# q in 112-row blocks, the last queries' scores on opposite array quarters, and three raw buffers for q, k and v

## The chip, the cores and the metric

The kernel runs on one core of a Trainium2 chip. The metric is the device time of one execution in microseconds; the median of three runs stands for the kernel. A core has five engines that each work through a list of their own: TensorE (PE, with its weight loads as PEld), VectorE (DVE), ScalarE (ACT), GpSimd (POOL) and SyncE (SP), which here issues every transfer between device memory and on-chip memory. They wait for one another by semaphores. Matmul results land in PSUM, which is divided into banks.

## The reference

Causal attention over 4 batches x 12 heads, 448 queries each, head width 64, followed by a two-layer block with a rational activation ("MoE" in the names), all float32 in the reference; the weights come in as float64.

```python
scores = scale * np.matmul(q, k.transpose(0, 1, 3, 2))      # (4, 12, 448, 448)
scores = np.where(mask, -1000000000.0, scores)
scores = scores - np.max(scores, axis=-1, keepdims=True)
attn = np.exp(scores)
attn = attn / (np.sum(attn, axis=-1, keepdims=True) + 1e-09)
x = (attn @ v).transpose(0, 2, 1, 3).reshape(1792, 768)
h = x @ w_in                                                 # d_ff = 2048
g = (a0 + a1*h + a2*h**2 + a3*h**3) / (1 + |b0|*|h| + |b1|*h**2 + 1e-6)
out = g @ w_out
```

## The kernel before

The kernel has two stages. In the first, attention, the 48 heads are taken in 24 pairs p; both heads of a pair go through together, 64 columns each. In the second the MoE block works through 64 units of tokens x hidden columns. The float64 weights are turned into float32 blocks (items m) already during attention, in small steps between the attention work.

The order of the work is written by hand. The string ORDER lists the tasks of one iteration; a name with `@2` is done for the pair two before the iteration's own, one with `@-1` for the pair one ahead. Each engine gets its instructions in that order, so a task that has to wait holds up what comes behind it on its engine. The tasks that matter here:

- `ld` (`stage_load`, L206 on) loads q and k of a pair, `@-3`: three pairs ahead. k goes in two loads (one a head) of 4 blocks of 112 rows into a tile with two buffers. q goes in four: for each head three blocks of 128 rows (L213), and the last 64 rows (L214) into the half of the partitions that belongs to the head. Its tiles R are two, used in turn, and their other half is cleared once at the start, so that the last 128 rows hold a block-diagonal q.
- `lv` (`stage_load_v`) loads v in three loads (L223 twice, L226) into one of two tiles V, `@1`: for the pair one before the iteration's own. `d` (`stage_d`, L358), which uses it, is `@2`.
- `qk` (`qk_pe`) transposes q and k on TensorE into two PSUM tiles, `@-1`; `qx`, `qy` and `kx`, `ky` copy them out on ScalarE (L253, L262).
- `s.3` (`stage_b_pe` with i = 3, L280) makes the scores of the last 64 queries of both heads in one product over all 128 rows; `s.2`, `s.1` and `s.0` make those of the others, one product for each head over 64 rows, into two banks. `m` subtracts masks and takes the maximum on VectorE (L292), `e` is the exponential on ScalarE (L299), `r` the reciprocal of the sums on VectorE (L310), `n` the normalising on GpSimd (L314).
- `c` transposes the weights of attention (L334), `a` and `v` copy them out (L342 on ScalarE, L344 on VectorE), `dh` and `dl` split the result into two parts (L368, L371).
- `cv` does the weight steps: on GpSimd (L130, L134) for the pair after, on VectorE (L138, L143), and `cv.3` on SP: it stores a finished float32 block (L149) and loads the float64 block after next (L116, L121) into the tile `raw`, which has two buffers. Pairs 1 to 4 do two of VectorE's steps, the later ones one, so that a store and a load come in every iteration at first and in every second one later.

SP's list in an iteration is thus: store and weight load (if any), v, q, k. The program gives each transfer one of eight lanes (`DMAHW0` to `DMAHW7`) in turn, and a transfer waits for the one before it on its lane.

Of the kernel before, what the change touches and what calls it, by code (L numbers as in the profile page):

```python
# [15 lines left out]


ORDER = """
c.1@2 e.3@1 cv.3 qk@-1 lv@1 e.0@1 v.1@2 dh@3 ld@-3 s.3 r@1 a.1@2 dl@3 n.5@1 qy@-1 c.0@2 m.6 kx@-1 n.4@1 ky@-1 s.2
qx@-1 v.0@2 n.0@1 a.0@2 s.1 n.2@1 e.6 m.5 n.1@1 s.0 m.4 d@2 n.3@1 e.5 m.0 n.6@1 m.2 e.4 m.3 cv.0@-1 e.2 m.1 cv.1  # L20
cv.2 e.1
"""
# [5 lines left out]
"""  # L28

TAIL = """  # L30
e.3@1 c.1@2 e.0@1 v.1@2 dh@3 lv@1 r@1 dl@3 a.1@2 n.5@1 n.4@1 c.0@2 xr n.2@1 n.3@1 v.0@2 a.0@2 n.6@1 wh.1.0 p1.0
n.0@1 n.1@1 wl.1.0 d@2 aa.0 da.0 wh.2.0 dz.0 ab.0 wl.2.0 c.1@1 v.1@1 a.1@1 dh@2 dl@2 c.0@1 a.0@1 v.0@1 p1.1 db.0 dy.0
lw.4.0 gh.0 gl.0 wh.0.1 wl.0.1 aa.1 da.1 d@1 p1.2 xl dh@1 dl@1 dz.1 ab.1 wh.1.1 wl.1.1 wh.3.0 lw.2.1 x.13.0 p2.0
lw.3.1 aa.2 lw.5.0 db.1 wl.3.0 dy.1 wh.4.0 wl.4.0
# [3 lines left out]
def kernel(  # L38
# [23 lines left out]
    SCALE = 1.0 / float(D) ** 0.5  # L62
# [141 lines left out]
    raw, K, AT, pv, SUM, REC, psa, pss, psc, nmx = {}, {}, {}, {}, {}, {}, {}, {}, {}, {}  # L204

    def stage_load(p):  # L206
        if p in raw:
            return
        b, hp = divmod(p, HP)
        t = R[p % 2]  # L210
        for j in range(2):
            src = q[b, 2 * hp + j]
            nc.sync.dma_start(out=t[:, :3, j], in_=src[:3 * P].rearrange("(c p) d -> p c d", p=P))  # L213
            nc.sync.dma_start(out=t[half(j), 3, j], in_=src[3 * P:])  # L214
        t = raw[p] = ld.tile([CP, NB, 2, D], F32, tag="k", name="kraw")
        for j in range(2):
            nc.sync.dma_start(out=t[:, :, j], in_=k[b, 2 * hp + j].rearrange("(c p) d -> p c d", p=CP))

    def stage_load_v(p):
        b, hp = divmod(p, HP)  # L220
        t = V[p % 2]
        for j in range(2):
            nc.sync.dma_start(  # L223
                out=t[:, j, :3], in_=v[b, 2 * hp + j, :3 * P].rearrange("(c p) d -> p c d", p=P)
            )
        nc.sync.dma_start(  # L226
            out=t[QB:, :, 3], in_=v[b, 2 * hp:2 * hp + 2, 3 * P:].rearrange("j p d -> p j d")
        )


    def half(j):
        return slice(j * D, (j + 1) * D)

    def ring(x, name):
        return ps_t.tile([P, 512], F32, tag=f"t{x}", bufs=3, name=name)

    def qk_pe(p):
        ps = psa[p] = [ring(x, "psA") for x in range(2)]
        for c in range(4):
            for x in range(2):  # L240
                r = slice(x * QB, (x + 1) * QB)
                nc.tensor.transpose(
                    ps[x][:, c * QB:(c + 1) * QB], R[p % 2][r, c].rearrange("p j d -> p (j d)"), ident[r, r]
                )
        for c in range(NB):
            for x, w in enumerate((QB, CP - QB)):
                r, lo = slice(x * QB, x * QB + w), 4 * QB + c * w
                nc.tensor.transpose(
                    ps[x][:, lo:lo + w], raw[p][r, c].rearrange("p j d -> p (j d)"), ident[r, r]
                )  # L250

    def q_ev(p, x):
        nc.scalar.activation(  # L253
            out=Q[p % 2].rearrange("p (c x r) -> p c x r", c=4, x=2)[:, :, x],
            in_=psa[p][x][:, :4 * QB].rearrange("p (c r) -> p c r", c=4), func=AF.Copy, scale=SCALE,
        )

    def k_ev(p, x):
        if p not in K:
            K[p] = qk.tile([P, S], F32, tag="k", name="kt")  # L260
        lo, hi = x * QB, (QB, CP)[x]
        nc.scalar.copy(  # L262
            out=K[p].rearrange("p (c r) -> p c r", c=NB)[:, :, lo:hi],
            in_=psa[p][x][:, 4 * QB:4 * QB + NB * (hi - lo)].rearrange("p (c r) -> p c r", c=NB),
        )

    b_w = (P, P, 2 * P, 2 * P, 3 * P, 3 * P, S)

    def stage_b_pe(p, i):
        w = b_w[2 * i]  # L270
        if i == 0:
            ps, lo = [pss[p, 2 + j][0] for j in range(2)], 2 * P
        else:
            ps = [ring(x, "psS") for x in range(2)] if i < 3 else [ps_s.tile([P, 512], F32, tag="s3", name="psS")]
            lo = 0
        for j in range(len(ps)):
            o = ps[j][:, lo:lo + w]
            pss[p, 2 * i + j] = (ps[j], o)
            d = half(j) if i < 3 else slice(None)
            nc.tensor.matmul(  # L280
                o, Q[p % 2][d, i * P:(i + 1) * P], K[p][d, :w], start=True, stop=True, skip_group_check=True
            )

    def stage_b_max(p, i):
# [68 lines left out]
    def stage_d(p):  # L353
        ps = pv[p] = ring(0, "psD") if p >= NP - 2 else ps_s.tile([P, 512], F32, tag="d", name="psD")
        a = [AT[p, h].rearrange("p n x q -> p (n x q)") for h in range(2)]
        v = V[p % 2]
        for j, c, h, slot, lo, hi in d_jobs:
            nc.tensor.matmul(  # L358
                ps[half(j), lo * QB:hi * QB], v[:, j, c], a[h][:, slot * QB:(slot + hi - lo) * QB],
                start=(c == 0 and lo == 0), stop=(c == 3), skip_group_check=True,  # L360
            )
# [205 lines left out]
    with tc.manual_schedule():  # L567
# [8 lines left out]
            out=mask[:, 2 * P:3 * P], in_=mask[:, 2 * P:3 * P], compare_op=ALU.is_ge, fill=-1e9, base=0,  # L576
            pattern=[[-1, P]], channel_multiplier=1,
        )
        for j in range(2):
            m = mask[half(j), 3 * P + S - QB:]  # L580
            nc.gpsimd.affine_select(
                out=m, in_=m, compare_op=ALU.is_ge, fill=-1e9, base=0, pattern=[[-1, QB]], channel_multiplier=1,
# [6 lines left out]
        lv = es_l.enter_context(pool(name="lv", bufs=2))  # L589
        ps_t = es_l.enter_context(pool(name="ps_t", bufs=1, space=PSUM))  # L590
        ld = es_r.enter_context(pool(name="ld", bufs=2, side="right"))
        qk = es_r.enter_context(pool(name="qk", bufs=2, side="right"))
        ps_s = es_r.enter_context(pool(name="ps_s", bufs=1, space=PSUM, side="right"))
        for x in ("s3", "d"):
            ps_s.tile([P, 512], F32, tag=x, name="psS")

        Q = [qk.tile([P, 512], F32, tag=f"q{x}", bufs=1, name=f"qt{x}") for x in range(2)]
        R = [ld.tile([P, 4, 2, D], F32, tag=f"q{x}", bufs=1, name=f"qraw{x}") for x in range(2)]
        V = [lv.tile([P, 2, 4, D], F32, tag=f"v{x}", bufs=1, name=f"vraw{x}") for x in range(2)]
        E = [  # L600
            [ep.tile([P, w], F32, tag=f"e{x}{i}", name=f"e{x}{i}") for i, w in enumerate(b_w)]
            for x in range(2)
        ]
# [110 lines left out]
```

## Time and profile before

| | |
|---|---|
| runs | 675.38, 676.63, 669.61 us; median 675.38 |
| the profiled execution | 678.74 us, its span 676.9 us |
| TensorE busy / weight loads | 633.1 us (94%) / 527.5 us (78%) |
| VectorE busy | 536.7 us (79%) |
| ScalarE busy | 427.0 us (63%) |
| GpSimd busy | 207.4 us (31%) |
| moved | 154.98 MB, 229 GB/s over the span |
| loads of q | 48 of 96 KB, 48 of 16 KB |
| loads of k | 48 of 112 KB |
| loads of v | 48 of 96 KB, 24 of 32 KB |
| loads of float64 weights | 32 of 768 KB |

The busy shares are averages over the two stages, which have different limits; what the change touches lies in attention, about the first 194 us. A row of the timeline or of the chain begins with its start and its length in us; a bracket at its end says how long the engine stood before it and for whom. "SPq" rows are the issuing of transfers: their length is that of the issue, not of the transfer.

### The profile page before, as it was taken

The page shows a single profiled execution, that of the slowest core. Times are in us where ns is not written, and L with a number is a line of the kernel's source. Part 1 is how long each engine was busy: PE and PEld are TensorE (multiplying, and loading weights), DVE is VectorE, ACT ScalarE, POOL GpSimd, SP SyncE. Part 2 cuts the span into 40 slices and gives each one's busy share as a digit, 9 for nine tenths or more (in the row PEclk, how much of TensorE's full clock was granted, in tenths as well). Part 3 has the DMA queues.
Part 4 walks back from the last instruction along what each step waited for, and adds up shares of the span by engine and source line. Part 5 has one row for each costly group of instructions (what it writes and reads, how often), then busy time and mean ns, then how long its engine had stood idle before and what let it go on. Part 6 is the DMA issues. An engine that isn't in the chain of part 4 may idle for free.

```text
span 676.9 us, 12813 instructions
## 1 busy us (share of the span) xinstructions
PE 633.1 (94%) x4560; PEld 527.5 (78%) x4560; DVE 536.7 (79%) x1036; ACT 427.0 (63%) x968; POOL 207.4 (31%) x269
## 2 busy tenths in 40 slices
PE   4888988787899998999999999999999999999997
PEld 2555755555577887788887888889999999999996
DVE  1897987887768999999999996866886557786654
ACT  3876987887775665655566656655564555764543
POOL 2667655665565555234355320000000000000000
PEclk9998998999999999999999999999999999999999
DMA  7687767667744898887788698864657785657763
GB/s 181 164 212 176 182 176 190 158 163 207 187 141 170 289 307 312 299 283 280 276 281 319 246 335 310 286 219 171 234 178 262 240 276 193 234 185 251 243 225 116
DMA packets 111679, 154.98 MB, mean 229 GB/s; under 512 B 71936, under 2 KB 84224, under 8 KB 111616
## 3 DMA queue, kind: packets, MB, share of 16 engines
q1 hardware_dynamic: 111616, 154.17, 70.1%
q8 instruction: 36, 0.59, 0.4%
q14 instruction: 27, 0.22, 0.1%
HBM read 117.18 MB, written 36.96 MB: 228 GB/s over the span
## 4 chain that ended last, share of the span: by engine, by line
PE 50%; DVE 27%; DMA 8%; issue 7%; POOL 3%; ACT 2%; SPq 1%; DVEq 0%; POOLq 0%; ACTq 0%
PE psH L196 21%; PE psO L508 16%; PE psM L509 8%; DMA vraw<-in_v_dram 3%; DVE u L138 3%; DVE psS L292 3%; DVE p L468 3%; DMA kraw<-in_k_dram 3%; DVE p L462 3%; DVE w L437 3%; POOL e L314 3%; DVE whl L179 2%; PE psD L358 2%; DVE w L459 2%; PE psS L280 2%
## 5 line engine op out<-in xcount | busy, mean ns | idle before, releaser
L196 PE MATMUL psH<-xh,whl 128*128 128x512 f32 (+1 forms) x768 | 175.9, 364 | 0.5 <-DVE p L445 0.5
L508 PE MATMUL psO<-whl,gh 128*128 128x512 f32 x448 | 160.9, 395 | 3.7 <-ACT gh L474 3.6
L196 PEld LDWEIGHTS psH<-xh,whl 128*128 128x128 f32 x768 | 136.0, 188 | 16.1 <-DVE p L445 0.9
L509 PE MATMUL psM<-whl,gh 128*128 128x256 f32 x448 | 126.2, 282 | 0.0
L508 PEld LDWEIGHTS psO<-whl,gh 128*128 128x128 f32 x448 | 84.0, 188 | 25.9 <-ACT gh L474 8.7
L452 ACT ACTIVATE u<-w,lnb 128x512 f32<-128x512 f32 (+1 forms) x64 | 43.0, 671 | 93.0 <-DVE w L437 93.0
L314 POOL TENSOR_SCALAR e<-e,r 128x384 f32<-128x384 f32 (+3 forms) x168 | 83.0, 516 | 55.4 <-DVE r L310 39.9
L299 ACT ACTIVATE e<-psS,nm 128x256 f32<-128x256 f32 (+3 forms) x168 | 82.6, 505 | 13.6 <-DVE nm L292 11.3
L292 DVE CUSTOM_DVE_ANT_0 psS<-psS,mask 128x128 f32<-128x128 f32 (+3 forms) x168 | 73.6, 473 | 18.7 <-PE psS L280 16.5
L196 PE MATMUL psH<-xl,whl 128*128 128x512 f32 (+1 forms) x384 | 87.4, 362 | 0.0
L509 PEld LDWEIGHTS psM<-whl,gh 128*128 128x128 f32 x448 | 84.5, 189 | 0.9
L508 PE MATMUL psO<-whl,gl 128*128 128x512 f32 x224 | 81.1, 391 | 0.0
L196 PEld LDWEIGHTS psH<-xl,whl 128*128 128x128 f32 x384 | 70.1, 188 | 7.5
L474 ACT CAST gh<-p 128x512 fp32r<-128x512 f32 (+1 forms) x64 | 36.8, 575 | 51.9 <-DVE p L468 51.9
L358 PE MATMUL psD<-at,vraw 128*64 128x64 f32 (+5 forms) x576 | 53.6, 325 | 16.2 <-DMA vraw<-in_v_dram 9.3
L280 PE MATMUL psS<-kt,qt 64*128 64x256 f32 (+3 forms) x336 | 67.3, 438 | 0.7 <-DVE at L344 0.2
L481 DVE TENSOR_TENSOR gl<-p,gh 128x384 fp32r<-128x384 f32 (+1 forms) x62 | 38.2, 616 | 35.1 <-ACT gh L474 35.1
L358 PEld LDWEIGHTS psD<-at,vraw 128*64 128x64 f32 x576 | 38.2, 142 | 32.4 <-ACT e L299 12.7
L509 PE MATMUL psM<-whl,gl 128*128 128x256 f32 x224 | 63.2, 282 | 0.0
L179 DVE TENSOR_TENSOR whl<-w,whl 128x768 fp32r<-128x768 f32 x45 | 45.6, 1014 | 21.4 <-ACT whl L171 20.9
L130 POOL TENSOR_SCALAR raw<-raw 128x768 f32<-128x768 f32 x32 | 38.0, 1186 | 80.2 <-DMA raw<-in_moe_w_in_dram 51.4
L430 ACT ACTIVATE u<-psH 128x512 f32<-128x512 f32 (+1 forms) x64 | 34.3, 535 | 44.0 <-PE psH L196 43.9
(56 smaller groups left out, 1049.2 us busy)
## 6 DMA issues: line engine op xcount, KB each, us to landing
whl<-whl SPq DMA_DIRECT2D x88, 768.0 KB, 4.2
w<-w SPq DMA_DIRECT2D x64, 384.0 KB, 5.1
raw<-in_moe_w_in_dram SPq DMA_DIRECT2D x16, 768.0 KB, 7.1
w<-u SPq DMA_DIRECT2D x32, 384.0 KB, 3.2
raw<-in_moe_w_out_dram SPq DMA_DIRECT2D x16, 768.0 KB, 6.0
kraw<-in_k_dram SPq DMA_DIRECT2D x48, 112.0 KB, 2.6
out_dram<-osb SPq DMA_DIRECT2D x14, 384.0 KB, 2.9
qraw<-in_q_dram SPq DMA_DIRECT2D x48, 96.0 KB, 4.1
```

The costliest lines, as they stand in the source:

```text
L130: nc.gpsimd.tensor_scalar(out=y, in0=y, scalar1=2.0 ** -112, scalar2=1.0, op0=ALU.mult, op1=ALU.mult)
L179: eng.tensor_tensor(out=w[:, 1], in0=src, in1=w[:, 0].bitcast(F32), op=ALU.subtract)
L196: nc.tensor.matmul(ps, w[:, c * P:(c + 1) * P], x[c][:, lo:lo + n_tok], start=(c == 0 and n == 0), stop=(c == KD - 1 and n == 2),)
L280: nc.tensor.matmul(o, Q[p % 2][d, i * P:(i + 1) * P], K[p][d, :w], start=True, stop=True, skip_group_check=True)
L292: nc.vector.tensor_tensor_reduce(out=s, in0=s, in1=m, scale=-1.0, scalar=3e38, op0=ALU.add, op1=ALU.min, accum_out=nmx[p][:, i:i + 1],)
L299: nc.scalar.activation(out=E[p % 2][i][:, :w], in_=pss[p, i][1], func=AF.Exp, bias=nmx[p][:, i:i + 1], scale=-1.0, accum_out=SUM[p][:, i:i ...
L314: nc.gpsimd.tensor_scalar(out=e, in0=e, scalar1=REC[p][:, i:i + 1], scalar2=0.0, op0=ALU.mult, op1=ALU.add)
L358: nc.tensor.matmul(ps[half(j), lo * QB:hi * QB], v[:, j, c], a[h][:, slot * QB:(slot + hi - lo) * QB], start=(c == 0 and lo == 0), stop=(c ...
L452: nc.scalar.activation(out=r, in_=w, func=AF.Ln, scale=2.0 ** -LSH, bias=lnb[:, 0:1])
L481: eng.tensor_tensor(out=gl, in0=pp, in1=gh.bitcast(F32), op=ALU.subtract)
L508: nc.tensor.matmul(acc[k], g, w[:, :512], start=first, stop=last)
L509: nc.tensor.matmul(m, g, w[:, 512:], start=first and k % 2 == 0, stop=last, skip_group_check=True)
```

## The change

q is loaded like k: two loads of four 112-row blocks, no separate last rows. q, k and v each have three buffers. `lv` loses its `@1` and goes out for the iteration's own pair. The two score products of the last 64 queries are taken apart: head 0 from rows 0 to 63 of the array to its columns 0 to 63, head 1 from rows 64 to 127 to columns 64 to 127, both into the one tile `s3`. The transposes of q take the shapes of those of k, the evictions read them with a shared helper `cut`, and the clearing of R is gone.

```diff
 ORDER = """
-c.1@2 e.3@1 cv.3 qk@-1 lv@1 e.0@1 v.1@2 dh@3 ld@-3 s.3 r@1 a.1@2 dl@3 n.5@1 qy@-1 c.0@2 m.6 kx@-1 n.4@1 ky@-1 s.2
+c.1@2 e.3@1 cv.3 qk@-1 lv e.0@1 v.1@2 dh@3 ld@-3 s.3 r@1 a.1@2 dl@3 n.5@1 qy@-1 c.0@2 m.6 kx@-1 n.4@1 ky@-1 s.2
...
 TAIL = """
-e.3@1 c.1@2 e.0@1 v.1@2 dh@3 lv@1 r@1 dl@3 a.1@2 n.5@1 n.4@1 c.0@2 xr n.2@1 n.3@1 v.0@2 a.0@2 n.6@1 wh.1.0 p1.0
+e.3@1 c.1@2 e.0@1 v.1@2 dh@3 r@1 dl@3 a.1@2 n.5@1 n.4@1 c.0@2 xr n.2@1 n.3@1 v.0@2 a.0@2 n.6@1 wh.1.0 p1.0
...
         b, hp = divmod(p, HP)
-        t = R[p % 2]
-        for j in range(2):
-            src = q[b, 2 * hp + j]
-            nc.sync.dma_start(out=t[:, :3, j], in_=src[:3 * P].rearrange("(c p) d -> p c d", p=P))
-            nc.sync.dma_start(out=t[half(j), 3, j], in_=src[3 * P:])
-        t = raw[p] = ld.tile([CP, NB, 2, D], F32, tag="k", name="kraw")
-        for j in range(2):
-            nc.sync.dma_start(out=t[:, :, j], in_=k[b, 2 * hp + j].rearrange("(c p) d -> p c d", p=CP))
+        raw[p] = {}
+        for n, src in (("q", q), ("k", k)):
+            t = raw[p][n] = ld.tile([CP, NB, 2, D], F32, tag=n, bufs=3, name=f"{n}raw")
+            for j in range(2):
+                nc.sync.dma_start(out=t[:, :, j], in_=src[b, 2 * hp + j].rearrange("(c p) d -> p c d", p=CP))
...
-        t = V[p % 2]
+        t = V[p % 3]
...
+        for n, src in enumerate(("q", "k")):
+            for c in range(NB):
+                for x, w in enumerate((QB, CP - QB)):
+                    r, lo = slice(x * QB, x * QB + w), (n * NB + c) * w
+                    nc.tensor.transpose(
+                        ps[x][:, lo:lo + w], raw[p][src][r, c].rearrange("p j d -> p (j d)"), ident[r, r]
+                    )
...
     def q_ev(p, x):
-        nc.scalar.activation(
-            out=Q[p % 2].rearrange("p (c x r) -> p c x r", c=4, x=2)[:, :, x],
-            in_=psa[p][x][:, :4 * QB].rearrange("p (c r) -> p c r", c=4), func=AF.Copy, scale=SCALE,
-        )
+        o, i = cut(Q[p % 2], psa[p], x, 0)
+        nc.scalar.activation(out=o, in_=i, func=AF.Copy, scale=SCALE)
...
+        elif i < 3:
+            ps, lo = [ring(x, "psS") for x in range(2)], 0
         else:
-            ps = [ring(x, "psS") for x in range(2)] if i < 3 else [ps_s.tile([P, 512], F32, tag="s3", name="psS")]
-            lo = 0
-        for j in range(len(ps)):
+            ps, lo = [ps_s.tile([P, 512], F32, tag="s3", name="psS")] * 2, 0
+        for j in range(2):
             o = ps[j][:, lo:lo + w]
             pss[p, 2 * i + j] = (ps[j], o)
-            d = half(j) if i < 3 else slice(None)
             nc.tensor.matmul(
-                o, Q[p % 2][d, i * P:(i + 1) * P], K[p][d, :w], start=True, stop=True, skip_group_check=True
+                o if i < 3 else o[half(j)], Q[p % 2][half(j), i * P:min((i + 1) * P, S)], K[p][half(j), :w],
+                start=True, stop=True, skip_group_check=True,
             )
...
-        for x in range(2):
+        for x in range(3):
             nc.gpsimd.memset(V[x][:QB, :, 3], 0.0)
-            for j in range(2):
-                nc.gpsimd.memset(R[x][half(j), 3, 1 - j], 0.0)
```

On SP, in the middle of attention, an iteration with a weight store and load stood so before (`raw` is the float64 weight block, `w_1_1` the stored one; a bracket names the lane and the engines that a transfer waits for):

```order
L149 DMA w_1_1_89<-u 128x768 [waits DMAHW6_49,DVE_49]
L121 DMA raw_1363<-in_moe_w_out_dram 128x1536 [waits DMAHW7_49,Pool_49]
L223 DMA vraw_200<-in_v_dram 128x3x64 [waits DMAHW0_49,PE_49]
L223 DMA vraw_200<-in_v_dram 128x3x64 [waits DMAHW1_49,PE_49]
L226 DMA vraw_200<-in_v_dram 64x2x64 [waits DMAHW2_49,PE_49]
L213 DMA qraw_198<-in_q_dram 128x3x64 [waits DMAHW3_49,PE_49]
L214 DMA qraw_198<-in_q_dram 64x64 [waits DMAHW4_49,PE_49]
L213 DMA qraw_198<-in_q_dram 128x3x64 [waits DMAHW5_49]
L214 DMA qraw_198<-in_q_dram 64x64 [waits DMAHW6_49,PE_49]
L217 DMA kraw<-in_k_dram 112x4x64 [waits DMAHW7_49,PE_49]
L217 DMA kraw<-in_k_dram 112x4x64 [waits DMAHW0_49]
```

The same place of SP's list now, on to the first load of the next iteration:

```order
L149 DMA w_1_1_89<-u 128x768 [waits DMAHW1_49,DVE_49]
L121 DMA raw_1359<-in_moe_w_out_dram 128x1536 [waits DMAHW2_49,Pool_49]
L220 DMA vraw_198<-in_v_dram 128x3x64 [waits DMAHW3_49,PE_49]
L220 DMA vraw_198<-in_v_dram 128x3x64 [waits DMAHW4_49,PE_49]
L223 DMA vraw_198<-in_v_dram 64x2x64 [waits DMAHW5_49,PE_49]
L214 DMA qraw<-in_q_dram 112x4x64 [waits DMAHW6_49]
L214 DMA qraw<-in_q_dram 112x4x64 [waits DMAHW7_49]
L214 DMA kraw<-in_k_dram 112x4x64 [waits DMAHW0_49]
L214 DMA kraw<-in_k_dram 112x4x64 [waits DMAHW1_49]
L220 DMA vraw_199<-in_v_dram 128x3x64 [waits DMAHW2_49,PE_49]
```

Two q loads are gone, the waits of q and k for TensorE are gone, and the load that shares the lane of the weight load (`DMAHW7` before, `DMAHW2` now) is no longer the iteration's first k load but the next iteration's first v load.

At the start of SP's list, the loads of the first two pairs stood so before the first weight block:

```order
L213 DMA qraw_198<-in_q_dram 128x3x64
L214 DMA qraw_198<-in_q_dram 64x64
L213 DMA qraw_198<-in_q_dram 128x3x64
L214 DMA qraw_198<-in_q_dram 64x64
L217 DMA kraw<-in_k_dram 112x4x64 x2
L213 DMA qraw_199<-in_q_dram 128x3x64
L214 DMA qraw_199<-in_q_dram 64x64
L213 DMA qraw_199<-in_q_dram 128x3x64 [waits DMAHW0_49]
L214 DMA qraw_199<-in_q_dram 64x64 [waits DMAHW1_49]
L217 DMA kraw<-in_k_dram 112x4x64 [waits DMAHW2_49]
L217 DMA kraw<-in_k_dram 112x4x64 [waits DMAHW3_49]
```

and stand so now:

```order
L214 DMA qraw<-in_q_dram 112x4x64 x2
L214 DMA kraw<-in_k_dram 112x4x64 x2
L214 DMA qraw<-in_q_dram 112x4x64 x2
L214 DMA kraw<-in_k_dram 112x4x64 x2
L116 DMA raw_230<-in_moe_w_in_dram 128x6x256 [waits DMAHW0_49]
```

Twelve loads have become eight, all without a wait.

On TensorE, `s.3` and the work behind it (`c.0`) stand so now, where one product 128x448 stood at L280 before:

```order
L240 MATMUL psA<-ident,kraw 128x64
L240 MATMUL psA<-ident,kraw 128x48
L275 MATMUL psS<-kt,qt_196 64x448 x2
L330 MATMUL psC<-ident,e_201 128x64 x2
L330 MATMUL psC<-ident,e_203 128x64 x2
```

The product has become two of 64 output rows; nothing else has changed its place there.

## Rows read from the trace of the kernel before

**Rows 1.** Busy time by stage: stretch, its length, busy us (instructions) of each engine.

```profile
core 0: us, PE busy (x) PEld busy (x) DVE busy (x) ACT busy (x) POOL busy (x), PEclk, DMA share, GB/s
18.63:66.20 47.57, 39.39 (x477) 26.80 (x476) 40.97 (x122) 35.99 (x125) 31.89 (x52) 0.96 0.73 187
66.20:171.12 104.92, 89.87 (x1205) 63.55 (x1204) 87.20 (x280) 87.63 (x298) 63.56 (x112) 0.98 0.69 178
171.12:194.06 22.94, 20.55 (x246) 14.27 (x245) 17.31 (x60) 17.51 (x60) 11.89 (x22) 0.93 0.73 206
194.06:676.90 482.84, 474.15 (x2573) 417.22 (x2571) 387.56 (x558) 278.29 (x468) 95.26 (x65) 1.00 0.71 247
```

**Rows 2.** The same view, three single iterations, from reciprocal to reciprocal.

```profile
66.20:72.25 6.05, 5.96 (x86) 4.25 (x86) 5.95 (x20) 5.85 (x22) 3.37 (x7) 1.00 0.86 247
100.11:110.28 10.17, 8.05 (x87) 5.43 (x86) 6.77 (x20) 7.05 (x25) 5.68 (x9) 0.83 0.69 174
177.27:188.03 10.76, 8.37 (x73) 5.09 (x72) 6.06 (x20) 7.52 (x24) 5.17 (x8) 0.84 0.81 233
```

**Rows 3.** Pieces of the chain of waits, 81 to 105 us.

```profile
81.81 6.77 DMA raw<-in_moe_w_out_dram
...
89.03 4.00 DMA kraw<-in_k_dram
...
97.52 7.21 DMA vraw<-in_v_dram
```

**Rows 4.** Timeline of TensorE, two of the attention-times-v products that waited.

```profile
104.86 3.84 PE L358 MATMUL psD<-at,vraw 128*64 128x448 f32 x24 [2.04 <-DMA vraw<-in_v_dram]
...
182.28 4.04 PE L358 MATMUL psD<-at,vraw 128*64 128x448 f32 x24 [2.31 <-DMA vraw<-in_v_dram]
```

**Rows 5.** Timeline of SP: an early place, then two iterations from store to store.

```profile
40.60 1.92 SPq L217 DMA_DIRECT2D kraw<-in_k_dram  x2
...
43.14 0.48 SPq L116 DMA_DIRECT2D raw<-in_moe_w_in_dram  x1
...
81.28 0.44 SPq L149 DMA_DIRECT2D w<-u  x1
81.81 0.38 SPq L121 DMA_DIRECT2D raw<-in_moe_w_out_dram  x1
...
88.64 0.87 SPq L217 DMA_DIRECT2D kraw<-in_k_dram  x2
...
95.33 1.08 SPq L217 DMA_DIRECT2D kraw<-in_k_dram  x2
96.50 0.44 SPq L149 DMA_DIRECT2D w<-u  x1
```

**Rows 6.** Timeline of an undisturbed iteration: products on half rows, half columns, the full array.

```profile
68.77 1.98 PE L358 MATMUL psD<-at,vraw 128*64 128x448 f32 x24
...
71.81 1.02 PE L280 MATMUL psS<-kt,qt 128*128 128x448 f32 x2
72.76 0.71 PE L334 MATMUL psC<-ident,e 64*128 64x64 f32 x16
...
73.00 0.62 DVE L292 CUSTOM_DVE_ANT_0 psS<-psS,mask 128x448 f32<-128x448 f32 x1
...
73.31 0.86 PE L280 MATMUL psS<-kt,qt 64*128 64x384 f32 x4
```

**Rows 7.** Two pieces of the chain of waits in an early iteration.

```profile
47.23 4.07 issue
51.35 0.89 POOL raw L130
```

**Rows 8.** Timeline of the start: issue of the second pair's k, its transposes, the first scores.

```profile
6.40 1.12 SPq L217 DMA_DIRECT2D kraw<-in_k_dram  x2
...
9.98 0.67 PE L248 MATMUL psA<-ident,kraw 64*128 64x64 f32 x8 [1.59 <-DMA kraw<-in_k_dram]
...
10.58 1.11 PE L280 MATMUL psS<-kt,qt 128*128 128x448 f32 x1
```

More of the change, by code (lines that the diff above doesn't have):

```diff
@@ L238, in qk_pe, with cut @@
         ps = psa[p] = [ring(x, "psA") for x in range(2)]
-        for c in range(4):
-            for x in range(2):
-                r = slice(x * QB, (x + 1) * QB)
-                nc.tensor.transpose(
-                    ps[x][:, c * QB:(c + 1) * QB], R[p % 2][r, c].rearrange("p j d -> p (j d)"), ident[r, r]
-                )
[L245 to L250, printed above, removed]
+        for n, src in enumerate(("q", "k")):
[5 more added lines that the diff above has]
+                    )
+    def cut(t, ps, x, n):
+        lo, hi = x * QB, (QB, CP)[x]
+        w = NB * (hi - lo)
+        return (
+            t.rearrange("p (c r) -> p c r", c=NB)[:, :, lo:hi],
+            ps[x][:, n * w:(n + 1) * w].rearrange("p (c r) -> p c r", c=NB),
+        )
     def q_ev(p, x):
-        nc.scalar.activation(
-            out=Q[p % 2].rearrange("p (c x r) -> p c x r", c=4, x=2)[:, :, x],
-            in_=psa[p][x][:, :4 * QB].rearrange("p (c r) -> p c r", c=4), func=AF.Copy, scale=SCALE,
-        )
+        o, i = cut(Q[p % 2], psa[p], x, 0)
+        nc.scalar.activation(out=o, in_=i, func=AF.Copy, scale=SCALE)
     def k_ev(p, x):
@@ L260, in k_ev @@
             K[p] = qk.tile([P, S], F32, tag="k", name="kt")
[L261 to L265, printed above, removed]
+        o, i = cut(K[p], psa[p], x, 1)
+        nc.scalar.copy(out=o, in_=i)
     b_w = (P, P, 2 * P, 2 * P, 3 * P, 3 * P, S)
@@ L355, in stage_d @@
         a = [AT[p, h].rearrange("p n x q -> p (n x q)") for h in range(2)]
-        v = V[p % 2]
+        v = V[p % 3]
         for j, c, h, slot, lo, hi in d_jobs:
@@ L595 @@
             ps_s.tile([P, 512], F32, tag=x, name="psS")
-        Q = [qk.tile([P, 512], F32, tag=f"q{x}", bufs=1, name=f"qt{x}") for x in range(2)]
-        R = [ld.tile([P, 4, 2, D], F32, tag=f"q{x}", bufs=1, name=f"qraw{x}") for x in range(2)]
-        V = [lv.tile([P, 2, 4, D], F32, tag=f"v{x}", bufs=1, name=f"vraw{x}") for x in range(2)]
+        Q = [qk.tile([P, S], F32, tag=f"q{x}", bufs=1, name=f"qt{x}") for x in range(2)]
+        V = [lv.tile([P, 2, 4, D], F32, tag=f"v{x}", bufs=1, name=f"vraw{x}") for x in range(3)]
         E = [
@@ L603 @@
         ]
-        for x in range(2):
+        for x in range(3):
             nc.gpsimd.memset(V[x][:QB, :, 3], 0.0)
-            for j in range(2):
-                nc.gpsimd.memset(R[x][half(j), 3, 1 - j], 0.0)
         def attend(p, part):
```

## The prediction

> **What bounds the kernel now.** I split the span at the reciprocal that each attention iteration does once (an iteration works on one pair of heads; there are 24) and read the busy time by stage [rows 1]. From 194 us on all is MoE: TensorE is busy 474 of 483 us, and the diff touches nothing there. What attention saves is therefore saved at the end, one for one. In attention no engine is full: between 66.20 and 171.12 us, 14 iterations, VectorE is busy 87.20 of 104.92 us, ScalarE 87.63, TensorE 89.87. Single iterations are of two kinds [rows 2]: one of 6.05 us in which VectorE is busy 5.95, and others of 10.17 and 10.76 us in which it does about the same work (6.77 and 6.06) and waits. So the floor is VectorE's and ScalarE's work, 87.20/14 = 6.23 us an iteration; the mean, 104.92/14 = 7.49, has 1.26 us of waiting on top.
>
> What is waited for stands in the chain: 6.77 us for a weight load, then 4.00 for a k load, then 7.21 for a v load [rows 3]. TensorE says the same: it stands 2.04 and 2.31 us before the attention-times-v products because v has not landed, and those products then take 3.84 and 4.04 us where an undisturbed set takes 1.98 [rows 4, 6].
>
> Why do loads come late that could be issued an iteration or two ahead? Because SP, which issues all of them, is late [rows 5]. Its list has two holds, both visible in the order rows of the change: each load waits for the lane of the load eight places before it, so at most eight are under way; and a q or k load waits for TensorE to have transposed the buffer's former content in the same iteration. In two iterations SP issues one weight store, one weight load and 18 loads of q, k and v. The weight load goes out at 81.81 us and lands 6.77 later; the eighth load behind it, the first k load, goes out at 88.64, just then. Ten more issues follow with little pause, and the next weight store comes at 96.50, right behind the last k loads of 95.33. That is a closed loop of 96.50 - 81.28 = 15.2 us for two iterations: the 7.49 us of the stage. SP's list is the bound.
>
> **The change part by part.**
>
> q in two loads in place of four, and free of TensorE. The loop becomes: store and weight load, then v, v, v, q, q, k, k behind it while it flies; the eighth behind it is now the next iteration's first v. After the landing seven issues are left in place of eleven. The eleven take 96.50 - 88.64 = 7.86 us, 0.71 each with their small waits; two k loads at 95.33 take 1.08, 0.54 each [rows 5]. New loop: 0.53 + 6.83 + 7 x 0.54 to 0.71 = 11.1 to 12.3 us. The floor of two iterations is 12.5 us, so the floor takes over, by little. I take 6.4 us an iteration, the floor plus 0.17 for waits that stay: 14 x (7.49 - 6.4) = 15.3 us. Bounds: 17.7 (the floor reached) and 8.7 (the weight load takes 8.2 us, as from 43.14 to 51.35 in [rows 5, 7], and issues stay at 0.71: 0.53 + 8.2 + 5.0 = 13.7 us, 6.87 an iteration).
>
> v an iteration earlier, into a third buffer. It goes out two iterations before its use, so the 7.21 us of its landing lie within 12. This removes the stop of the last iterations: 177.27 to 188.03 takes 10.76 us [rows 2] for work of 6.4, so 4.4 us. The third buffer's own wait, for the products of three pairs before, was met an iteration ago when SP comes to it, so nothing stands behind it. Bounds 3 to 5.
>
> The first iterations, 18.63 to 66.20 us, six, four of them with two weight steps each. There the chain goes through the weight load itself: GpSimd ends its normalising at 47.23, the chain shows 4.07 us of nothing, and the next weight block starts at 51.35, 8.2 us after its load was issued at 43.14; that issue came behind the k loads of 40.60, which took 1.92 us in place of 1.08 [rows 5, 7]. With two q loads gone no k load stands in the way, but the next weight store becomes the one that waits for the weight load's lane, so an iteration stays a landing plus about 1 us. VectorE's idle time there is 47.57 - 40.97 = 6.6 us [rows 1]. I take half, 3.5; bounds 0 and 6.
>
> The start. The second pair's k transposes run at 9.98 us, 2.5 us behind the end of their issue (6.40 + 1.12), and the first scores start at 10.58 [rows 8]. Eight issues stand there in place of twelve: 4 x 0.54 = 2.2 us earlier. The clearing of the q buffers on GpSimd goes too, hidden behind the wait for q here. I take 2.3; bounds 1 and 3.
>
> The last 64 queries' scores. One product over all 128 rows and columns becomes two, head 0 on one quarter of the array and head 1 on the opposite one, both of 448 columns, into the two halves of one PSUM bank. The trace has no such quarter; the nearest rows bound it [rows 6]. Products on the upper and lower half rows, into two banks, overlap: twice 384 columns in 0.86 us. Products on the left and right half columns overlap even in one bank: twice 1024 columns in 1.98 us, against 448 in 1.02 on the full array. The quarters are both patterns at once, and their outputs lie as those of the half columns. I take 0. The other end is one after the other. From 1024 in 1.98 and 448 in 1.02, 448 columns stream for 0.75 us; with its start not hidden a product costs the 0.95 from 71.81 to TensorE's next work at 72.76. VectorE takes the scores at 73.00, 0.17 us after they end at 72.83. So 0.58 to 0.78 us an iteration, 23 times: 13 to 18 us.
>
> That end has a page on its side, the strongest against this change: the Trainium skill, page "TensorEngine Tiling (Array Packing)", section "Restrictions and Gotchas" (Gotcha 1), says that different row tiles cannot access the same PSUM bank at the same time. The quarters are different row tiles on one bank. By that rule the sum below would be about 10 us, by the rows 25; no row of before shows row tiles on one bank.
>
> The second eviction of q has 192 columns in place of 256, so ScalarE gets a little less work. I count 0: the floor above is VectorE's too.
>
> **The sum.** 15.3 + 4.4 + 3.5 + 2.3 = 25.5 us. The profiled execution's own time is 678.74 us, its span 676.9 and 1.8 around it: 653.2. The median of the runs shown, 675.38, is 3.4 lower; I put that down to such waits, which mostly go, and subtract a third of it: 652.
>
> **The rivals.** Their times have the same 1.2 us taken off.
>
> Quarters in turn. 13 to 18 us come back, 7.5 to 12.5 stay: 665 to 670. For it: the bank is shared. Against: half columns share one and overlap. (It is what the page's rule would make of this kernel.)
>
> Half relief. SP's loop stays the bound, since the weight load lands later when more loads share the queue: 8.7 in place of 15.3, 2 in place of 3.5, so 17.4 us: 660. For it: the new loop is only 0.2 to 1.4 us shorter than the floor. Against: the bytes of an iteration are the same, and the 6.05 us iteration moved 247 GB/s where the stage's mean is 178 [rows 1, 2].
>
> No relief. The loads are late because the DMA engines can do no more, and lists and buffers don't matter. Only the start gains: 675. Against it is the same 247 GB/s.
>
> Slower. q, k and v, no longer held by TensorE, crowd the weight loads, and GpSimd, which does its weight step between two normalisings, stands for each as for the 4.07 us in [rows 7]. One weight load comes every two iterations, eight after 66 us; at 4.07 each that is 32.6 us, 7 more than the 25.5: 685. It decides from 25.5/8 = 3.2 us a load. Against it: with the shorter list SP comes to the weight load earlier, not later.
>
> **How the numbers follow.** Forecast (645 to 657) 0.54; half relief (657 to 664) 0.16; quarters in turn 0.16, half of it past the one per cent; no relief 0.07; slower 0.07. One per cent, 6.75 us, is about what a measurement of this kernel can tell from no change; faster by more means below 668.6. Faster 0.54 + 0.16 + 0.08 = 0.78; within 1% 0.08 + 0.07 = 0.15; slower 0.07. The range: the low end takes away all of VectorE's idle time after the first reciprocal, 6.6 + 17.7 + 5.6 = 29.9, and the start: 645. The high end takes in the quarters in turn: 670. Left out are no relief, slower and the tails.
>
> **What would show it.** Right: iterations after 66 us of 6.1 to 6.6 us with VectorE busy 6.0 to 6.4; SP standing at the weight store for VectorE; v and k gone from the chain; TensorE's next work still about 0.95 us behind the quarter products. Wrong: quarter products of about 1.9 us together (in turn); the first v load of an iteration going out late and products waiting for v or k (half or no relief); GpSimd standing before its weight step (slower). All of it falls if the MoE stage, 482.84 us, does not keep its length.

## The result, and the profile after

The changed kernel takes 649.45 us (median of four runs, 648.2 to 653.25) where the kernel before takes 674.18 (four runs beside it): a ratio of 0.965, 95% interval 0.958 to 0.972. The prediction was 652, in a range of 645 to 670. The profiled execution of the changed kernel took 649.19 us, its span is 647.4.

The span by stages, cut at the same reciprocals as in [rows 1] (stretch, length, busy us and instructions of each engine, granted clock, DMA share, GB/s):

```profile
core 0: us, PE busy (x) PEld busy (x) DVE busy (x) ACT busy (x) POOL busy (x), PEclk, DMA share, GB/s
0.00:16.26 16.26, 9.32 (x70) 5.57 (x72) 3.68 (x17) 7.51 (x25) 4.38 (x15) 1.00 0.93 219
16.26:58.23 41.97, 38.22 (x488) 25.78 (x486) 40.88 (x123) 35.17 (x124) 33.53 (x52) 0.96 0.91 215
58.23:144.38 86.15, 86.13 (x1234) 58.06 (x1232) 84.09 (x281) 83.13 (x295) 63.85 (x112) 1.00 0.90 217
144.38:164.19 19.81, 18.56 (x250) 12.67 (x249) 18.05 (x60) 17.65 (x61) 11.95 (x22) 1.00 0.73 219
164.19:647.40 483.21, 474.56 (x2573) 417.13 (x2571) 387.96 (x558) 278.52 (x468) 96.50 (x65) 1.00 0.70 247
```

Against [rows 1] the start is 2.4 us shorter (18.63 to 16.26), the first six iterations 5.6 (47.57 to 41.97), the fourteen in the middle 18.8 (104.92 to 86.15), the last three 3.1 (22.94 to 19.81), and MoE keeps its length (482.84, now 483.21). That is 29.5 us between the two profiled executions; the medians are 24.7 apart, because the profiled execution of before, 678.74 us, was longer than all four of its runs.

In the middle stage iterations of 5.96 and 6.34 us now alternate, without the stops of 10 us [rows 2], and the waits for v, k and weight loads [rows 3, 4] are gone: of TensorE's idle time between 16 and 170 us none is put down to a load. SP's list over two iterations (start, length of the issue):

```profile
82.01 0.35 SPq L149 DMA_DIRECT2D w<-u  x1
82.46 0.39 SPq L116 DMA_DIRECT2D raw<-in_moe_w_in_dram  x1
82.94 1.28 SPq L220 DMA_DIRECT2D vraw<-in_v_dram  x2
84.31 0.61 SPq L223 DMA_DIRECT2D vraw<-in_v_dram  x1
84.97 1.12 SPq L214 DMA_DIRECT2D qraw<-in_q_dram  x2
86.13 1.71 SPq L214 DMA_DIRECT2D kraw<-in_k_dram  x2
87.94 2.11 SPq L220 DMA_DIRECT2D vraw<-in_v_dram  x2
...
91.96 1.02 SPq L214 DMA_DIRECT2D kraw<-in_k_dram  x2
94.31 0.35 SPq L149 DMA_DIRECT2D w<-u  x1
```

Where SP in [rows 5] took 15.2 us from store to store and had nothing left over, it is now through its list at 92.98, after 11.0 us, and stands 1.3 us for the next block to store. The view of waits, 16 to 170 us, says for whom (us in total, times, longest):

```profile
SPq L149 <- DVE u L143: 19.1, 11, 2.3
```

In the middle stage the chain of waits now runs along TensorE alone. Over one iteration (a later section shows that the other engines are nearly level with it):

```profile
88.34 0.90 PE psS L275 x4
89.24 0.64 PE psC L330 x16
89.88 1.59 PE psS L275 x12
91.48 1.91 PE psD L354 x20
93.39 0.64 PE psC L330 x16
94.03 0.49 PE psA L240 x15
```

And the two quarter products, in TensorE's timeline, stand where one product of 1.02 us stood in [rows 6]; the next work follows 0.90 us after their start, 0.95 before:

```profile
69.82 0.97 PE L275 MATMUL psS<-kt,qt 64*64 64x448 f32 x4
70.72 0.71 PE L330 MATMUL psC<-ident,e 64*128 64x64 f32 x16
```

### The profile page after: what moved, and what is told of

Its sections match the earlier page's. It is cut to its first block, busy times and chain, and to the rows that moved or that the text cites. A ratio compares the mean times of both kernels' runs of the same rounds, so it can differ in the third digit from the quotient of the medians.

```text
span 647.4 us, 12773 instructions
## 1 busy us (share of the span) xinstructions
PE 626.8 (97%) x4608; PEld 519.2 (80%) x4608; DVE 534.7 (83%) x1036; ACT 422.0 (65%) x968; POOL 210.2 (32%) x266
## 4 chain that ended last, share of the span: by engine, by line
PE 65%; DVE 24%; issue 6%; ACT 3%; POOL 1%; SPq 1%; DMA 0%; DVEq 0%; ACTq 0%; POOLq 0%
PE psH L196 22%; PE psO L504 16%; PE psM L505 8%; PE psS L275 8%; PE psD L354 5%; PE psC L330 4%; DVE u L138 3%; DVE p L464 3%; DVE w L433 3%; DVE p L458 3%; DVE whl L179 2%; DVE w L455 2%; DVE gl L477 2%; DVE psS L288 2%; DVE p L436 2%
## 5 line engine op out<-in xcount | busy, mean ns | idle before, releaser
L310 POOL TENSOR_SCALAR e<-e,r 128x384 f32<-128x384 f32 (+3 forms) x168 | 81.1, 508 | 37.4 <-DVE r L306 30.7
L295 ACT ACTIVATE e<-psS,nm 128x256 f32<-128x256 f32 (+3 forms) x168 | 83.5, 518 | 13.3 <-DVE nm L288 11.1
L275 PE MATMUL psS<-kt,qt 64*128 64x384 f32 (+3 forms) x384 | 69.3, 460 | 0.5 <-ACT at L338 0.2
L477 DVE TENSOR_TENSOR gl<-p,gh 128x384 fp32r<-128x384 f32 (+1 forms) x62 | 39.9, 644 | 35.0 <-ACT gh L470 35.0
L130 POOL TENSOR_SCALAR raw<-raw 128x768 f32<-128x768 f32 x32 | 40.1, 1253 | 65.6 <-DMA raw<-in_moe_w_in_dram 39.4
L179 POOL TENSOR_TENSOR whl<-w,whl 128x768 fp32r<-128x768 f32 x19 | 40.6, 2138 | 46.9 <-ACT whl L171 43.2
L433 DVE SCALAR_TENSOR_TENSOR w<-w,bb,u 128x512 f32<-128x512 f32 (+1 forms) x64 | 50.6, 791 | 5.7 <-ACT w L427 5.7
```

The costliest lines, as they stand in the source:

```text
L130: nc.gpsimd.tensor_scalar(out=y, in0=y, scalar1=2.0 ** -112, scalar2=1.0, op0=ALU.mult, op1=ALU.mult)
L179: eng.tensor_tensor(out=w[:, 1], in0=src, in1=w[:, 0].bitcast(F32), op=ALU.subtract)
L275: nc.tensor.matmul(o if i < 3 else o[half(j)], Q[p % 2][half(j), i * P:min((i + 1) * P, S)], K[p][half(j), :w], start=True, stop=True, ski ...
L295: nc.scalar.activation(out=E[p % 2][i][:, :w], in_=pss[p, i][1], func=AF.Exp, bias=nmx[p][:, i:i + 1], scale=-1.0, accum_out=SUM[p][:, i:i ...
L310: nc.gpsimd.tensor_scalar(out=e, in0=e, scalar1=REC[p][:, i:i + 1], scalar2=0.0, op0=ALU.mult, op1=ALU.add)
L433: nc.vector.scalar_tensor_tensor(out=w, in0=w, scalar=bb[:, 0:1], in1=u, op0=ALU.add, op1=ALU.mult)
```

## Experiments: which part of the change is it?

**The quarters alone.** The kernel before, with the last 64 queries' scores in two quarter products and nothing else changed.

```diff
-            ps = [ring(x, "psS") ...] if i < 3 else [ps_s.tile([P, 512], F32, tag="s3", name="psS")]
+            ps = [ring(x, "psS") ...] if i < 3 else [ps_s.tile([P, 512], F32, tag="s3", name="psS")] * 2
...
-                o, Q[p % 2][d, i * P:(i + 1) * P], K[p][d, :w], ...
+                o if i < 3 else o[half(j)], Q[p % 2][half(j), qs], K[p][half(j), :w], ...
```

> The kernel before with one part of the change: the last 64 queries' scores on opposite quarters (q still block-diagonal, its zero halves unread). The trace of after shows the pair of quarter products in 0.97 us where the full product took 1.02. Theory: SP's loop still bounds attention, so the 24 x 0.05 us are hidden: 674 as before, within 2 us. Rival (the quarters themselves are part of the gain because TensorE is the bound): 1 to 5 us faster.

Measured: 676.02 us, 1.0007 times the kernel before (0.998 to 1.003). The two quarters neither cost nor give anything beyond 2 us here; but in this kernel SP's loop could hide a cost, so their price is measured once more below, where nothing hides it.

**The buffers alone.** The kernel before with three buffers for q, k and v and v's loads an iteration earlier; q still in four loads.

```diff
-... qk@-1 lv@1 e.0@1 ...
+... qk@-1 lv e.0@1 ...
...
-        t = R[p % 2]
+        t = R[p % 3]
...
-        t = raw[p] = ld.tile([CP, NB, 2, D], F32, tag="k", name="kraw")
+        t = raw[p] = ld.tile([CP, NB, 2, D], F32, tag="k", bufs=3, name="kraw")
...
-        t = V[p % 2]
+        t = V[p % 3]
...
```

> The kernel before with three buffers for q, k and v and v an iteration earlier, but q still in four loads (11 issues after the weight load's landing stay, and the eighth load behind it is still the first k load). Theory of the loop (the lanes and the length of SP's list bound it): the loop stays near 15 us for two iterations, only the stop for v near the end goes: 666 to 672. Rival (the holds for TensorE and late v were the cause): most of the gain comes, 650 to 656.

Measured: 676.2 us, 1.002 (1.000 to 1.004). That is far from the rival's range, but above the theory's too: the loop stayed, SP's stores come 15.1 us apart on average (66.59 to 157.36, six loops), and the stop for v near the end, which was to go, did not. The middle and the last stage of its profile:

```profile
66.56:166.94 100.38, 89.72 (x1187) 62.23 (x1186) 87.61 (x280) 85.62 (x296) 62.80 (x112) 0.97 0.71 182
166.94:191.85 24.91, 21.58 (x263) 14.67 (x264) 18.43 (x59) 18.09 (x62) 12.75 (x23) 0.93 0.71 202
```

A buffer more, and a place in the list that is an iteration earlier, do not help a list that is itself late.

**The buffers taken back.** The changed kernel with two buffers for q, k and v and v's loads at their old place; and, as a second kernel, with v alone taken back.

```diff
-... qk@-1 lv e.0@1 ...
+... qk@-1 lv@1 e.0@1 ...
...
-            t = raw[p][n] = ld.tile([CP, NB, 2, D], F32, tag=n, bufs=3, name=f"{n}raw")
+            t = raw[p][n] = ld.tile([CP, NB, 2, D], F32, tag=n, bufs=2, name=f"{n}raw")
...
-        t = V[p % 3]
+        t = V[p % 2]
...
```

> The changed kernel with two buffers for q, k and v and v loaded for the pair before, as it was; q in two loads and the quarters stay. Theory of the loop: 16 transfers in two iterations in place of 20, and the first v behind the landing, so most of the gain stays: 652 to 660. Rival (holds and late v): only the start's 2 us come, 668 to 673.

> The changed kernel with v's two buffers and its place for the pair before put back; q and k keep three buffers. Theory of the loop: v goes out about an iteration before its use and lands in 6 us, so it is rarely late: 649 to 655. Rival (late v was the stop): the stops for v come back, 2 us or more every second iteration, 665 or more.

Measured: 649.5 us (0.965, 0.960 to 0.970) with all buffers taken back, 649.21 us (0.964, 0.959 to 0.968) with v alone: the whole gain is still there, more of it than the theory had named for two buffers. So the gain belongs to q's loads. The buffers may still give the list some slack: the profiled execution with two buffers, the longest of its four runs, has two stops in the middle stage, which takes 90.88 us, against 86.18 with v alone taken back, and SP stands only 1.5 us there for VectorE's block at the store, against 7.9 with v alone taken back and 9.4 in the changed kernel. No difference of the medians shows it.

## Experiments: is it the number of loads?

**Four q loads of the new shape.** The changed kernel with q's load of each head taken apart, so that two iterations have 20 transfers again; **and three**, with one head's load taken apart: 18 transfers.

```diff
             for j in range(2):
-                nc.sync.dma_start(out=t[:, :, j], in_=src[b, 2 * hp + j].rearrange("(c p) d -> p c d", p=CP))
+                s = src[b, 2 * hp + j].rearrange("(c p) d -> p c d", p=CP)
+                for lo, hi in ((0, 3), (3, 4)) if n == "q" else ((0, 4),):
+                    nc.sync.dma_start(out=t[:, lo:hi, j], in_=s[:, lo:hi])
```

(For three the condition is `n == "q" and j`.)

> The changed kernel with each head's q load taken apart again into blocks 0 to 2 and block 3, so that SP issues 20 transfers in two iterations as before the change; the shape of q's tiles (112 rows), the three buffers, the early v load and the quarters stay. Loop theory (the number of transfers behind the weight load sets the pace): the two-iteration loop goes back from 12.3 to about 15 us, SP no longer stands for VectorE at the weight store, TensorE waits again for loaded data: 668 to 677 us. Rival (something else of the new q load gave the gain: its 112-row shape, the clearing gone, TensorE's transposes): 649 to 655 us.

> The changed kernel with the q load of one head of each pair taken apart (blocks 0 to 2, block 3) and that of the other whole: 18 transfers in two iterations, between the 16 of the changed kernel and the 20 of the kernel before. If SP's time for its list grows with the number of transfers (14.5 us in two iterations at 20, at most 10.3 of work at 16), 18 stand near 12.8 us, just over the 12.3 of the engines: 650 to 658 us. If it is a matter of whole or split q loads and not of the count: 668 or more, or 649.

Measured: 673.17 us with four (0.996, 0.993 to 0.999), 664.62 with three (0.982, 0.978 to 0.986). Same bytes, same shape, same quarters and buffers as in the changed kernel; two issues more in each iteration take nearly everything back. The middle stages of the two, four loads first:

```profile
63.99:165.26 101.27, 93.15 (x1232) 63.29 (x1232) 86.56 (x281) 84.99 (x295) 63.88 (x112) 0.93 0.75 186
```

```profile
61.58:153.22 91.64, 87.88 (x1214) 59.39 (x1212) 85.00 (x280) 83.60 (x295) 62.39 (x112) 0.96 0.79 197
```

| transfers in two iterations | store to store on SP, mean us | middle stage, us | median, us |
|---|---|---|---|
| 20 (before) | 15.4 | 104.9 | 674 to 676 |
| 20 (q in four loads, new shape) | 14.5 | 101.3 | 673.2 |
| 18 (q in three) | 13.8 | 91.6 | 664.6 |
| 16 (the change) | 12.3, with SP standing for VectorE | 86.2 | 649.5 |

From SP's own 11.0 us at 16 transfers to 14.5 at 20 is 0.9 us a transfer, an issue with its waits: with four loads the view of waits has 10.0 us of SP waiting for a weight load to land in the middle stage, 1.4 in each of its seven loops, and in the changed kernel none. The loop need not be much over the 12.3 us of the engines to cost: the loads go out up to three iterations ahead, and a loop that is too long uses this lead up a little in each round. With three q loads the iterations are 5.96 to 6.33 us as in the changed kernel up to 98 us; the first stop, 10.85 us, comes between 111.58 and 122.43. The expectation for 18, 650 to 658, took the loop 1.0 us too short (12.8, measured 12.4 to 15.3, 13.8 on average) and the time 7 us too low. Seven such loops make up the middle stage, so the longer loop could account for this alone; the expectation also left out what each such stop costs beyond the lateness itself. The two were not told apart.

The cost of a stop can be read in the kernel with four loads, whose TensorE stands for a k load and goes on slower (timeline, then the granted clock of stretches before and after the wait):

```profile
79.54 0.66 PE L242 MATMUL psA<-ident,kraw 64*128 64x64 f32 x8 [2.45 <-DMA kraw<-in_k_dram]
80.13 1.76 PE L277 MATMUL psS<-kt,qt 64*64 64x448 f32 x4
81.82 1.12 PE L332 MATMUL psC<-ident,e 64*128 64x64 f32 x16
82.73 2.87 PE L277 MATMUL psS<-kt,qt 64*128 64x384 f32 x12
...
88.74 0.97 PE L277 MATMUL psS<-kt,qt 64*64 64x448 f32 x4
89.64 0.72 PE L332 MATMUL psC<-ident,e 64*128 64x64 f32 x16
90.18 1.53 PE L277 MATMUL psS<-kt,qt 64*128 64x384 f32 x12
```

```profile
73.00:77.40 4.40, 3.87 (x56) 2.96 (x56) 4.32 (x16) 4.19 (x17) 4.28 (x7) 1.00 0.71 150
79.54:82.90 3.36, 3.36 (x30) 1.87 (x32) 0.69 (x2) 1.10 (x4) 1.73 (x4) 0.50 0.68 168
82.93:85.60 2.67, 2.67 (x16) 1.65 (x16) 1.83 (x5) 1.75 (x5) 0.00 (x0) 0.50 0.88 170
```

TensorE stood 2.45 us; then it ran at half its clock, 1.2 GHz, until past 85.60. The same three groups took 1.76, 1.12 and 2.87 us, at full clock 0.97, 0.72 and 1.53: 2.5 us more, as much as the wait itself.

## Experiments: what makes SP's loop long?

**Weight loads off SP's list, and then the stores too.** The kernel before, q still in four loads, with the 768 KB loads of the float64 weights issued by GpSimd; in a second kernel also the 384 KB stores.

```diff
-            nc.sync.dma_start(
+            nc.gpsimd.dma_start(
                 out=raw.rearrange("p (c f) t -> p c (f t)", c=KD),
...
-            nc.sync.dma_start(
+            nc.gpsimd.dma_start(
                 out=raw.rearrange("p m t -> p (m t)"), ...
```

```diff
-        nc.sync.dma_start(out=w32[items[m]], in_=c_32[m])
+        nc.gpsimd.dma_start(out=w32[items[m]], in_=c_32[m])
```

> The kernel before with one thing changed: the float64 weight loads are issued by GpSimd and not by SP, so that they no longer stand in SP's list nor on its eight lanes. q keeps its four loads, 19 transfers in two iterations are left on SP. Theory (the eighth load behind a weight load stands for that load's landing, 6.8 us or more): the standing goes, 19 issues at 0.54 to 0.71 us are 10.3 to 13.5 us for two iterations, so the middle stage comes near the 12.3 us that the changed kernel has: 652 to 664 us. Rival (the number of issues on SP, or the bytes, set the pace whoever issues the weight loads): 668 to 677 us. GpSimd spends some time on issuing, which both leave out.

> The kernel before with both long transfers of the conversion, the 768 KB weight loads and the 384 KB stores, issued by GpSimd. SP's list holds 18 loads of q, k and v in two iterations and nothing that lands later than about 4 us. With the weight loads alone moved away SP took 12.3 to 15.2 us for 19 transfers, while its unhindered issues add up to 11.0. If the landing of the long transfers that stay in the list (the store, 6.0 us there) is what held it: 10.6 to 11 us for 18, below the engines' 12.3: 652 to 660 us. If the number of loads, with bytes that land as slowly as they do, holds it: 13 us and more, 665 to 675.

Measured: 670.06 us (0.990, 0.987 to 0.993) and 683.69 us (ten runs, 676.8 to 692.6; 1.010, 1.006 to 1.015, without the two longest). As times, both are outside of what the theory had named: the first lies in the rival's range, the second above both. The stages say why. Issuing on GpSimd costs elsewhere: the first reciprocal comes at 22.22 and 23.66 us in place of 18.63, and MoE takes 485.89 and 494.81 us in place of 482.84. In the middle stage, where the theory speaks, both are faster than before by 9.5 and 11.0 us: 95.39 and 93.89 us in place of 104.92. With the weight loads gone from the list (19 transfers left) SP's stores are 12.3 us apart at first and 13.2 to 15.2 later:

```profile
66.90 0.35 SPq L149 DMA_DIRECT2D w<-u  x1
...
79.24 0.35 SPq L149 DMA_DIRECT2D w<-u  x1
...
94.05 0.41 SPq L149 DMA_DIRECT2D w<-u  x1
```

and the iterations keep to 6.1 us for as long as the lead lasts, to 98 us, and then no more:

```profile
67.77:98.44 30.67, 29.95 (x421) 20.70 (x420) 29.99 (x101) 29.63 (x105) 23.59 (x42) 1.00 0.80 201
98.44:163.16 64.72, 58.21 (x781) 40.59 (x782) 55.18 (x180) 55.69 (x191) 43.36 (x78) 0.97 0.74 190
```

With the stores gone too (18 loads left, all of q, k and v) ten iterations in a row take 6.23 us, with q still in four loads:

```profile
64.59:126.91 62.32, 61.31 (x851) 42.35 (x849) 60.61 (x201) 59.35 (x209) 51.76 (x90) 1.00 0.80 196
```

So SP's loop has two parts, and neither alone is the whole: the number of issues, and the long transfers among them that hold a lane. The prediction had only the weight load as such a holder; taking it away is not enough, since the store (6.0 us from issue to landing in that run, median; k loads wait 3.4 us for stores to land in the middle stage) and the number remain. What first stops the kernel without long transfers at 127 us is not settled: TensorE stands 1.46 us for a q load there and then 1.73 for a k load, which takes 6.8 us from issue to landing, while the weights, now issued by GpSimd, move at the same time.

## Experiments: what bounds the changed kernel, and the price of the quarters

**The quarters twice.** The changed kernel with the pair of quarter products done twice in a row into the same place.

```diff
             pss[p, 2 * i + j] = (ps[j], o)
+        for j in range(2) if i < 3 else (0, 1, 0, 1):
+            o = pss[p, 2 * i + j][1]
             nc.tensor.matmul(
```

> The changed kernel with the pair of quarter products done twice in a row into the same place (the second overwrites the first with the same scores). It prices a quarter pair and tells which engine now sets the pace of an iteration. If TensorE does (its chain through an iteration adds up to 6.1 us of 6.15): the second pair costs its whole length, 0.75 to 0.9 us in 24 iterations, 18 to 21 us: 667 to 671. If VectorE and ScalarE do, as the prediction had it: a part of it is taken by TensorE's slack, 649 to 660.

Measured: 658.27 us (0.974, 0.968 to 0.979), 8.8 over the changed kernel: inside the range named for VectorE and ScalarE setting the pace, near its upper end. TensorE's timeline shows a full iteration without any pause:

```profile
94.55 1.72 PE L277 MATMUL psS<-kt,qt 64*64 64x448 f32 x8
96.20 0.71 PE L332 MATMUL psC<-ident,e 64*128 64x64 f32 x16
96.75 1.52 PE L277 MATMUL psS<-kt,qt 64*128 64x384 f32 x12
98.20 1.98 PE L356 MATMUL psD<-at,vraw 128*64 128x448 f32 x24
100.11 0.71 PE L332 MATMUL psC<-ident,e 64*128 64x64 f32 x16
100.66 0.41 PE L240 MATMUL psA<-ident,qraw 64*128 64x64 f32 x8
100.90 0.41 PE L240 MATMUL psA<-ident,kraw 48*128 48x48 f32 x8
101.24 1.72 PE L277 MATMUL psS<-kt,qt 64*64 64x448 f32 x8
```

94.55 to 101.24 is 6.69 us, and 61.92 to 148.74, thirteen iterations, is 6.68 each: with the second pair TensorE sets the pace. Two pairs of quarters take 1.65 us to the next work, one pair 0.90: a further pair costs 0.75, which is what 448 columns cost once (the prediction's 0.75), not twice. So the two quarters run beside each other, and without the second pair TensorE's list alone would be 6.69 - 0.75 = 5.94 us. The changed kernel's iteration is 6.15 (86.15/14) with VectorE busy 6.01 (84.09/14) and ScalarE 5.94 (83.13/14). None of the three is the bound by itself; they are nearly level, and the 0.14 us above the fullest are waits between them, although the chain of waits shows TensorE alone. A second pair took first the 0.2 us by which the iteration is longer than TensorE's list, and cost the other 0.53.

**Weight steps spread out.** The changed kernel's first iterations take 7.4 to 7.65 us; four of them do two weight steps each.

```diff
     def quota(p):
-        return 2 if 1 <= p < 5 else int(5 <= p < NP - 1)
+        return int(1 <= p < NP - 1) + int(p in (4, 9, 14, 19))
```

> The changed kernel with VectorE's weight steps spread out: one step for each pair from 1 to 22 and a second one at pairs 4, 9, 14 and 19, in place of two at each of pairs 1 to 4 and one after. The same 26 steps. If the first iterations (7.4 to 7.6 us against 6.15 later) are long because two steps, VectorE's and GpSimd's at the same time, crowd them: each early iteration gets about 1 us shorter, and four later ones about 0.8 longer: 647 to 649. If they are long because of the landing of weight loads or the sum of work counts alone: 649 to 651, no change.

Measured: 654.48 us (0.966, 0.961 to 0.972 times the kernel before): above both expectations, and no gain on the changed kernel's 0.965. The first six iterations took 41.57 us (41.97 without the edit), since the first of them became longer, 8.78 us, behind a q load for which TensorE had stood 3.01 us, and the middle stage, with the weight loads at new places, got stops again and took 94.11 us. GpSimd's timeline shows one of them: a weight step that waits for its load, and a normalising held up behind it and stretched from 3.37 to 4.86 us.

```profile
127.91 3.37 POOL L310 TENSOR_SCALAR e<-e,r 128x384 f32<-128x384 f32 x7 [0.52 <-PE psS L275]
134.48 0.90 POOL L130 TENSOR_SCALAR raw<-raw 128x768 f32<-128x768 f32 x1 [3.20 <-DMA raw<-in_moe_w_out_dram]
...
136.33 4.86 POOL L310 TENSOR_SCALAR e<-e,r 128x384 f32<-128x384 f32 x7
```

This is the slower rival's mechanism, GpSimd standing for a weight load until the other engines wait too. In the changed kernel GpSimd stands for a weight load only in the first six iterations, three times for 0.7 to 1.4 us, and never in the middle stage. No version here beats the changed kernel by more than the noise.

## Why the prediction was right, and where not

**SP's list is the bound, and fewer q loads lift it: shown.** Four loads of the new shape bring the old loop back, three lie between, and two hold without the new buffers. The new loop was put at 11.1 to 12.3 us; SP's own part of it is 11.0. What the loop is made of was read right only in part. The prediction built both loops on one load's wait for the weight load's landing. In the middle stage of before this wait comes to 6.8 us (view of waits, us in total, times, longest):

```profile
SPq L217 <- DMA raw<-in_moe_w_out_dram: 4.6, 3, 1.5
SPq L217 <- DMA raw<-in_moe_w_in_dram: 2.2, 3, 0.9
```

That is about 1.0 us of a loop of 15.4, and less than half of what the stage gained. In the changed kernel the same view has no wait of SP for a weight load: the one issued at 82.46 lands 5.3 us later, at 87.8, and the seven issues behind it keep SP busy until 87.84, so that the next load goes out at 87.94 without standing for it. The new loop of 11.0 us is sixteen issues of 0.69 on average, with the small waits in them. So of the 4.4 us by which SP's list got shorter the number of issues is the larger part; the weight load taken away did not mend the loop. The rival by which the DMA engines can do no more falls too: the middle stage now moves 217 GB/s where it moved 178 [rows 1].

**The middle stage: mechanism right, 15.3 us taken, 18.8 found**, above the bound of 17.7. The floor of 6.23 us was VectorE's and ScalarE's busy time of before divided by 14, and this is no constant: it fell to 84.09 and 83.13 us, and the iteration to 6.15. VectorE's instructions did not get shorter by that much: by the view of lines (count times mean length, summed) they are 107.9 us long together in the middle stage of before and 107.4 in that of the changed kernel, while the busy time, which counts overlapping instructions once, fell by 3.1. So where the engine does not stop, its instructions overlap more. The floor also left TensorE out, whose busy time in [rows 1] (89.87) is inflated by its waits and by half clock, so that its true list, 5.94 us, could not be read there; it turned out level with the others.

**v an iteration earlier: the wrong edit.** 4.4 us stood for the third v buffer. The stage gave 3.1, but without that buffer it gives the same: the last three iterations take 19.94 us with v taken back. They take 19.94 as well with the quarters alone, with before's list, and 24.91 with the buffers alone; the stop is where a late list happens to show. And the interval taken to have 6.4 us of work has 7.82 (150.34 to 158.16; 7.82 also with four q loads), so that at most 2.9 of 10.76 could go.

**First iterations: 3.5 taken, 5.6 found**, inside the bounds of 0 to 6. What gave it was not taken apart; in the other kernels with whole q loads and the same order of weight steps the six iterations took 42.29 us (two buffers), 44.19 (v taken back) and 45.05 (quarters twice). **Start: 2.3 taken, 2.4 found**; the second pair's k transposes now run at 7.72 us, the first scores at 8.32, where [rows 8] has 9.98 and 10.58.

**The quarters: 0 taken, 0 found.** The next work is 0.90 us behind in place of 0.95. The rule in the Trainium skill, page "TensorEngine Tiling (Array Packing)", section "Restrictions and Gotchas" (Gotcha 1), that different row tiles cannot access one PSUM bank at the same time, is not what these two products show: two quarters into the two halves of one bank took 0.75 us a pair when repeated, the time of one.

**The sum came out well in part by luck.** Against the stages of the two profiled executions it is 4.0 us short, 25.5 for 29.5: the middle stage gave 3.5 more than taken, the first iterations 2.1 more and the start 0.1 more, the last iterations 1.3 less, and MoE took 0.4 more. Against the medians it is 0.8 over, 25.5 for 24.7, because the profiled execution of before lay 4.6 us above the median of its four runs. That the 652 came within 3 us of 649.45 rests on this too.

## What to carry to other kernels

When loads are late that could have gone out long before, look at the engine that issues them: count its transfers in one round, time it from one fixed instruction to the next, and compare that with the engines' own time. A loop only a little too long shows first as nothing, until the lead is used up, and then as stops that also cost TensorE its clock; more buffers do not mend it, fewer and larger transfers do. To learn which engine bounds a balanced stage, give one of them a known piece of extra work and see how much of it arrives.

## What was not expected of the hardware

- A stop of TensorE cost about twice its length in the three stops of over 2 us that were looked at. With four q loads it ran at 1.2 GHz until past 85.60 after 2.45 us of standing, and three groups of products took 5.75 us in place of 3.22. The two stops of the kernel before in [rows 4], 2.04 and 2.31 us, were followed by products 1.86 and 2.06 us longer than an undisturbed set, and the clock of their iterations was 0.83 and 0.84 [rows 2]. The prediction shows these lengths and drew nothing from them.
- Two quarter products of 448 columns on opposite quarters of the array, into the two halves of one PSUM bank, run beside each other: 0.97 us for the pair, 0.75 for each further one.
- The same small loads land later when the list moves faster: a k load took 2.5 us from issue to landing in the middle stage of before and 3.8 in that of the changed kernel (medians), at 178 and 217 GB/s, and it did no harm there.
